# A linear-attention and gated-unit kernel: stages split by engine and issued from a table, with another order of loads

## The chip, the cores and the metric

One NeuronCore of one Trainium2 chip runs the whole kernel. The metric is device time in microseconds (us), the median over runs. A profiled run also has a span, from its first to its last instruction; the device time is some 1.8 us longer (109.45 for a span of 107.7). PE is the matmul engine (PEld its weight loads), DVE the Vector engine, ACT the Scalar engine, POOL is GpSimd, SP the engine that issues the transfers.

A run counts as slow when it is over 1.5% above the fastest of the same kernel; ratios use fast runs alone. To evacuate a result means here to copy it from where PE leaves it into a tile that the next step reads.

## The reference

A recurrent attention (state decayed by `w`, bonus `u`) over 768 steps, 4 batches and 8 heads of 48, then a gated unit with a causal convolution of width 5:

```python
for t in range(S):
    cur = einsum('bhd,bhe->bhde', u * kt, vt)
    y[:, :, t] = einsum('bhd,bhde->bhe', rt, state + cur)
    state = w * state + einsum('bhd,bhe->bhde', kt, vt)
# x = y as [batch, seq, 384]
gate = sigmoid(causal_conv5(x, conv_w))
out  = (gate * (x @ w_val)) @ w_out          # float32
```

## The kernel before

The sequence is cut into twelve units of 256 tokens (three per batch), each of two chunks of 128. A unit loads r, k, v (393 KB each), scales r and k by powers of the decay, transposes them on PE, makes the attention matrix A (`attn`) and masks it, the bonus scalars s and dv = s * v, the state, and then the output `y_out`. I call the start of that output **Y** of the unit. Convolution, gate, value and projection of a unit follow its Y, mixed with the next unit's attention.

Every engine executes its instructions in the order in which the program emits them. A stage function emits the PE work and at once its evacuation or its product:

```python
    def transp_r(n, ps=(0, NP)):
        ...                                   # 8 PE transposes into tr
        nc.scalar.copy(out=st["rT", n]..., in_=tr)
    def mask_at(n, cl):
        for par in range(2):
            nc.vector.tensor_tensor(out=st["at", n, cl][:, par], ..., op=ALU.mult)
    def bonus_v(n):
        nc.gpsimd.tensor_tensor(out=dv_t[n % 2]..., in0=v_st[n]..., in1=st["s", n]..., op=ALU.mult)
```

The start-up is written out by hand, with `warm` matmuls (results thrown away) to keep the PE clock up. The loads come first in the order r0 k0 v0 k1 r1 k2 Wv v1 Wo r2 k3 v2 r3 k4 v3 (Wv, Wo: weights). The part between Y of unit 1 and Y of unit 2:

```python
    y_out(1)
    project(0, 8)                             # the second number: warming matmuls
    conv(1)
    scale_k(3, nc.gpsimd)
    transp_r(2)
    prod(2)
    value(1, 6)
    for cl in range(U):
        attn(2, cl, 6 - 6 * cl)
        mask_at(2, cl)
    bonus(2)
    bonus_v(2)
    transp_k(3)
    ...
    state(2, 0, 6)
    ...
    # units 3 to 12: a loop of the same calls; all stores come after the last load
```

## Time and profile before

| | before |
|---|---|
| device time, median of 3 (lowest, highest) | 109.53 us (109.05, 109.62) |
| Y of units 0, 1, 2, 3, 11 | 15.83, 24.39, 38.07, 45.99, 98.72 us |
| span of the profiled run | 107.7 us |

(The prediction dates units 2 and 3 by the chain of waits, 0.07 us later than PE's own timeline does.)

The prediction below shows the page's busy sums, the chain and the stretches. Two more views say what happens in the long gap between Y of units 1 and 2. First the totals of who waited for whom (engine, line and tile that waited, what it waited for: us in all, times, longest):

```profile
POOL dv L327 <- DVE s_sb L324: 25.8, 7, 8.1
DVE pr L298 <- ACT rT L253: 13.0, 11, 3.2
```

Then the timeline in that gap (start, length, engine, line, operation; in brackets the idle time before and what ended it):

```profile
30.31 0.69 DVE L298 TENSOR_TENSOR pr<-tr_ps,rT 128x1024 bf16<-128x1024 bf16 x1 [3.15 <-ACT rT L253]
...
30.92 1.01 DVE L500 TENSOR_TENSOR hT<-at_ps,gate 128x384 bf16<-128x384 f32 x2
...
31.85 2.47 DVE L355 TENSOR_TENSOR at<-at_ps,mask 128x512 bf16<-128x512 f32 x4
...
34.24 0.17 DVE L324 COPY s_sb<-kv_ps 128x16 f32<-128x16 f32 x1
...
34.48 2.12 POOL L327 TENSOR_TENSOR dv<-v_st,s_sb 128x768 bf16<-128x768 f32 x1 [8.14 <-DVE s_sb L324]
```

DVE idles 3.15 us for the evacuated r of unit 2. Then the gated value, four masks and s stand in line, and POOL has waited 8.14 us for that s. Those waits are one queue in program order.

The long wait of POOL is not the one that ends last, though: dv was done at 36.60, and the chain of waits goes from s over PE alone to Y of unit 2:

```profile
34.32 0.09 DVE s_sb L324
34.46 0.80 PE kv_ps L138 x6
...
35.93 0.85 PE at_ps L248 x8
36.78 1.36 PE at_ps L516 x6
38.14 1.26 PE mm_ps L414 x80
```

PE ran this part cold: its granted clock was 0.50 from 34.03 to 37.44 us, and the last two pieces before Y (the transposes of r3 and a projection) took 0.85 and 1.36 us, where the steady units show 0.45 and 0.97.

### The profile page before, as it was taken

To read this page: it belongs to the slowest core of one execution; us is meant where nothing else is said; L and a number is where in the kernel's file an instruction comes from. 1 tells how busy PE (TensorE), PEld (TensorE's weight loads), DVE (VectorE), ACT (ScalarE), POOL (GpSimd) and SP (SyncE) were. 2 spreads that over 40 slices of the span, in tenths; PEclk is the share of its full clock that TensorE was granted. 3 is DMA by queue.
4 is the path that set the end of the run, shared out by engine and by line. 5 is a ranking of instruction groups with operands and counts; after the bars stand their busy time and mean duration, and the time that the engine had idled before them with its cause. 6 is when DMAs were issued, how large, how long until landed. Compare 5 with 4: busy or idle time off the path is not lost.

```text
span 107.7 us, 5253 instructions
## 1 busy us (share of the span) xinstructions
PE 94.0 (87%) x2320; PEld 76.4 (71%) x2320; DVE 71.3 (66%) x137; ACT 73.2 (68%) x120; POOL 61.1 (57%) x62
## 2 busy tenths in 40 slices
PE   4999559979965979797999999999999999999860
PEld 4696447857844768586788797788978788785720
DVE  4295894789079326876689496975968789595030
ACT  4179556694826396495787987779878796973540
POOL 7851959077001990695945959679297894105000
PEclk9999999999998599999999999999999999999996
DMA  0999998989889899897979869797999994040404
GB/s 9 224 213 224 215 287 213 312 142 195 173 154 217 164 239 193 178 246 148 245 147 226 159 114 262 139 252 156 238 245 328 359 366 138 10 152 0 152 0 146
DMA packets 67347, 20.41 MB, mean 190 GB/s; under 512 B 63478, under 2 KB 67324, under 8 KB 67324
## 3 DMA queue, kind: packets, MB, share of 16 engines
q1 hardware_dynamic: 66492, 20.07, 79.6%
q8 instruction: 18, 0.29, 1.2%
q10 hardware_dynamic: 832, 0.00, 0.4%
q14 instruction: 5, 0.04, 0.1%
HBM read 15.35 MB, written 4.72 MB: 186 GB/s over the span
## 4 chain that ended last, share of the span: by engine, by line
PE 59%; ACT 11%; DVE 10%; DMA 8%; issue 5%; SPq 3%; DVEq 0%
PE mm_ps L462 11%; PE mm_ps L414 10%; PE at_ps L516 10%; DMA r_st<-in_r_dram 8%; DVE at L355 6%; ACT rT L253 5%; PE at_ps L248 5%; PE at_ps L483 5%; PE at_ps L342 4%; PE kv_ps L373 3%; PE tr_ps L284 3%; ACT xT L442 3%; PE kv_ps L382 2%; PE at_ps L492 2%; SPq L71 2%
## 5 line engine op out<-in xcount | busy, mean ns | idle before, releaser
L327 POOL TENSOR_TENSOR dv<-v_st,s_sb 128x768 bf16<-128x768 f32 x12 | 18.4, 1530 | 31.6 <-DVE s_sb L324 25.8
L355 DVE TENSOR_TENSOR at<-at_ps,mask 128x512 bf16<-128x512 f32 x48 | 29.9, 683 | 6.9 <-PE at_ps L342 6.9
L260 POOL TENSOR_TENSOR ks<-k_st,dk 128x768 bf16<-128x768 f32 x11 | 20.1, 1828 | 3.8 <-DMA k_st<-in_k_dram 3.8
L253 ACT COPY rT<-at_ps 128x1024 bf16<-128x1024 bf16 (+1 forms) x13 | 15.8, 1230 | 9.2 <-PE at_ps L248 9.2
L500 DVE TENSOR_TENSOR hT<-at_ps,gate 128x384 bf16<-128x384 f32 x24 | 12.5, 555 | 5.8 <-PE at_ps L492 5.5
L298 DVE TENSOR_TENSOR pr<-tr_ps,rT 128x1024 bf16<-128x1024 bf16 x11 | 7.6, 692 | 13.0 <-ACT rT L253 13.0
L289 ACT COPY kT<-tr_ps 128x1024 bf16<-128x1024 bf16 x11 | 11.1, 1012 | 6.7 <-PE tr_ps L284 6.7
L471 ACT ACTIVATE gate<-mm_ps 128x384 bf16<-128x384 f32 x24 | 10.5, 488 | 6.6 <-PE mm_ps L462 6.2
L234 POOL TENSOR_TENSOR rs<-r_st,dr 128x768 bf16<-128x768 f32 x8 | 14.6, 1830 | 0.0
L516 PE MATMUL at_ps<-wout,hT 128*128 128x384 bf16 x72 | 14.4, 334 | 0.2 <-DVE hT L500 0.2
L462 PE MATMUL mm_ps<-xT,cwd 64*64 64x256 bf16 (+1 forms) x500 | 12.7, 241 | 1.7 <-ACT xT L442 0.9
L462 PEld LDWEIGHTS <-cwd 64*64 64x64 bf16 x500 | 11.5, 106 | 3.2 <-issue 1.7
L523 ACT COPY o_sb<-at_ps 128x384 f32<-128x384 f32 x24 | 10.7, 493 | 3.6 <-PE at_ps L516 3.6
L442 ACT CAST xT<-mm_ps 128x384 bf16<-128x384 f32 x24 | 11.4, 493 | 1.8 <-PE mm_ps L414 1.3
L398 DVE TENSOR_TENSOR z<-kv_ps,wcm 128x384 bf16<-128x384 f32 x20 | 11.0, 549 | 1.5 <-PE kv_ps L382 1.5
L483 PE MATMUL at_ps<-xT,wval 128*128 128x256 bf16 x72 | 11.8, 272 | 0.0
L269 ACT CAST vb<-v_st 128x768 bf16<-128x768 f32 x12 | 10.2, 847 | 0.0
L516 PEld LDWEIGHTS <-hT 128*128 128x128 bf16 x72 | 6.3, 100 | 4.6 <-DVE hT L500 1.9
L414 PE MATMUL mm_ps<-at,vb 128*32 128x128 bf16 x384 | 9.6, 219 | 0.0
L248 PE MATMUL at_ps<-ident,rs 128*128 128x128 bf16 x96 | 8.2, 235 | 1.2 <-DVE rs L234 1.2
L342 PE MATMUL at_ps<-rT,kT 48*128 48x128 bf16 x192 | 8.1, 220 | 0.6 <-DVE hT L500 0.6
L414 PE MATMUL mm_ps<-ident,dv 128*32 128x128 bf16 x288 | 8.2, 219 | 0.0
(78 smaller groups left out, 149.8 us busy)
## 6 DMA issues: line engine op xcount, KB each, us to landing
r_st<-in_r_dram SPq DMA_DIRECT2D x12, 384.0 KB, 5.1
k_st<-in_k_dram SPq DMA_DIRECT2D x24, 192.0 KB, 5.0
v_st<-in_v_dram SPq DMA_DIRECT2D x24, 192.0 KB, 4.5
out_dram<-o_sb SPq DMA_DIRECT2D x11, 384.0 KB, 4.6
wv_st<-in_moe_w_val_dram SPq DMA_DIRECT2D x1, 576.0 KB
wo_st<-in_moe_w_out_dram SPq DMA_DIRECT2D x1, 576.0 KB, 5.5
out_dram<-o_sb SPq DMA_DIRECT2D x2, 192.0 KB, 1.9
wt<-in_w_dram ACTq DMA_DIRECT2D x2, 0.8 KB, 2.5
```

Of the source, the lines that this page charges most:

```text
L234: eng.tensor_tensor(out=rs_t[n % 2][:, :, ps[0] : ps[1], :, 0:D].rearrange("p s n a d -> p (n a) s d"), in0=r_st[n][:, hs], in1=dr[:, hs], ...
L248: nc.tensor.transpose(tr[:, s, p, :], rs_t[n % 2][:, s, ps[0] + p].rearrange("p a x -> p (a x)"), ident,)
L253: nc.scalar.copy(out=st["rT", n][:, ps[0] : ps[1], :].rearrange("x n (i s) -> x s n i", s=2), in_=tr,)
L260: eng.tensor_tensor(out=ks_t[n % 3][:, cs, :, :, 0:D].rearrange("p c n a d -> p c (n a) d"), in0=k_st[n][:, cs], in1=dk[:, None, :, :].to_ ...
L327: nc.gpsimd.tensor_tensor(out=dv_t[n % 2].rearrange("p c (h d) -> p (c h) d", d=D), in0=v_st[n].rearrange("p c h d -> p (c h) d"), in1=st[ ...
L355: nc.vector.tensor_tensor(out=st["at", n, cl][:, par], in0=st["at_ps", n, cl][par], in1=mask[:, None, :].to_broadcast([128, NP, 128]), op= ...
L414: nc.tensor.matmul(out=y_ps[32 * q : 32 * q + 32, T, :], lhsT=lt, rhs=rh, start=q not in first, stop=last, skip_group_check=True,)
L442: nc.scalar.copy(out=xT_t[b % 2][:, :, t0 : t0 + C], in_=y_ps)
L462: nc.tensor.matmul(out=g_ps[i][64 * qo : 64 * qo + 64, o0 : o0 + n0], lhsT=cwd[rows, T, t, :], rhs=xT[rows, T, t0 + c0 + t : t0 + c0 + t + ...
L483: nc.tensor.matmul(out=v_ps[:, 0:W], lhsT=wval[:, kt, i, :], rhs=xT[:, kt, t0 : t0 + W], start=(kt == 0), stop=(kt == NT - 1), skip_group_ ...
L500: nc.vector.tensor_tensor(out=hT[:, i], in0=v_ps, in1=st["gate", n][:, i], op=ALU.mult)
L516: nc.tensor.matmul(out=o_ps, lhsT=hT[:, i, c0 : c0 + C], rhs=wout[:, k, :], start=(j == 0), stop=(j == 2),)
```

## The change

The intent is to separate what each stage does on each engine, so that a table of tokens can place the PE part, the evacuation and the product independently, and to load r2 early. `RT:2.0` is the transposes of r of unit 2, `RE:2.0` their evacuation, `M:2.3` the fourth mask, and so on. A name ending in D (`DVD`) runs on DVE instead of POOL; by this r of unit 2 goes from DVE to POOL. The diff, cut to its core:

```diff
-    load_kv(1, "k")
-    load_r(1)
-    load_kv(2, "k")
 ...
     def transp_r(n, ps=(0, NP)):
         ...
+        st["r_tr", n, ps[0]] = tr
+
+    def evac_r(n, ps=(0, NP)):
         nc.scalar.copy(...)
 ...                                            (every stage is cut in this way)
+    LOADS = """
+        r0 k0 v0 r1 r2 k1 k2 Wv v1 Wo k3 r3 v2 r4 v3 k4 k5 r5 v4 v5 r6 k6 v6 r7 k7 k8 v7 r8 k9 v8
+        r9 k10 v9 r10 k11 v10 r11 v11
+    """
+    HEAD = """
+        CV:0.0 PR:0.0 A:0.1 M:0.3 S:0.0 RSD:1.0 RS:2.0 SE:0.0 M:0.2 A:0.0 KV:0.0~20 TL:0.0 ZE:0.0
+        RT:1.0 M:0.1 RT:2.0 RE:1.0 KS:1.0 RE:2.0 KV:0.1 ID:0.1 DVD:0.0 KT:1.0 KS:2.0 WV:0.0 ZE:0.1
+        Y:0.1 M:0.0 KE:1.0 Y:0.0 PR:1.0 YE:0.1 YE:0.0 A:1.1 S:1.0 C:0.0 A:1.0 KT:2.0 M:1.3 SG:0.0
 ...
+    STEP = """
+        Y:-1.0 Y:-1.1 A:0.0 YE:-1.0 RS:1.0 A:0.1 M:0.0 YE:-1.1 CV:0.0 C:-1.0 M:0.1 S:0.0 SG:-1.1
+        M:0.2 KS:1.0 M:0.3 SG:-1.0 V:-1.1 RT:1.0 V:-1.0 SE:0.0 KV:0.0 ID:0.0 HT:-1.1 KT:1.0
+        HT:-1.0 RE:1.0 O:-1.0 DV:0.0 ZE:0.0 KV:0.1 O:-1.1 ID:0.1 KE:1.0 OE:-1.0 ZE:0.1 OE:-1.1
+        PR:1.0
+    """
 ...
+    def issue():
+        while loads:
 ...
+                if old >= 0 and any((e, old, 0) not in seen for e in need):
+                    return
 ...
+        while stores and {("OE", stores[0], 0), ("OE", stores[0], 1)} <= seen:
+            store(stores.pop(0))
```

Of the 71 warming matmuls 20 remain (`KV:0.0~20`). Units 0 to 3 are in HEAD; STEP is repeated for each later unit; a short TAIL ends it.

## The prediction

> **What bounds the kernel now.** I read the page first, then the chain of waits in order of time, then busy time by stretch, then the timeline. The work comes in twelve units of 256 tokens. I date a unit by the start of its first output matmul (L414, called Y below).
>
> From the page of the kernel before: busy sums, then busy tenths in 40 slices of 2.69 us.
>
> ```profile
> PE 94.0 (87%) x2320; PEld 76.4 (71%) x2320; DVE 71.3 (66%) x137; ACT 73.2 (68%) x120; POOL 61.1 (57%) x62
> ...
> PEclk9999999999998599999999999999999999999996
> DMA  0999998989889899897979869797999994040404
> ```
>
> PE is fullest, yet DMA is at eight or nine tenths from 11 us until about 88 us. So two resources are near their limit, and an average cannot say which binds where. The clock dips in one place only (32 to 38 us).
>
> The chain of waits in order of time separates the stages (start, length, what). This is its middle:
>
> ```profile
> 29.08 1.20 ACT rT L253
> 30.35 0.57 issue
> 30.92 0.31 DVE hT L500
> ...
> 31.93 0.78 DVE at L355 x2
> 32.71 0.33 issue
> 33.04 1.28 DVE at L355 x2
> ...
> 73.37 1.23 PE mm_ps L414 x80
> 74.60 0.55 PE at_ps L342 x16
> 75.18 1.02 PE mm_ps L462 x40
> ```
>
> From about 46 us to 99 us the chain is almost unbroken PE. Near 30 us it hops between ACT, DVE and issue: PE waits there for results. The timeline gives Y of unit 0 at 15.83, unit 1 at 24.39, unit 2 at 38.14, unit 3 at 46.06 and unit 11 at 98.72 us. Hence gaps of 8.56, 13.75 and 7.92 us, then eight units in 52.66, or 6.58 us each, and 8.98 us of tail. Busy time in the last four of these stretches (us and its sum, PE, PEld, DVE, ACT, POOL, clock, DMA share, GB/s):
>
> ```profile
> 24.39:38.14 13.75, 11.51 (x228) 8.90 (x231) 8.18 (x12) 7.15 (x11) 5.61 (x4) 0.88 0.87 183
> 38.14:46.06 7.92, 6.71 (x192) 5.52 (x195) 4.65 (x9) 5.55 (x10) 4.10 (x4) 1.00 0.95 207
> 46.06:98.72 52.66, 51.12 (x1437) 42.41 (x1436) 40.87 (x78) 41.71 (x72) 36.22 (x22) 1.00 0.81 199
> 98.72:107.70 8.98, 4.96 (x159) 3.54 (x158) 1.05 (x2) 3.37 (x8) 0.00 (x0) 0.89 0.25 89
> ```
>
> PE is 97% busy in the steady stretch (51.12 of 52.66) and only 84% in the one before unit 2, at a clock of 0.88, with throwaway warming matmuls inside. Three units from 15.83 to 46.06 take 30.2 us where three steady ones take 19.7: **the start-up wastes some 10 us**, and the 13.75 us gap has most of it.
>
> **What the Trainium skill says.** (1) "TensorE: Matmul & The Clock Gate", HAM oscillation: an idle PE falls back to half clock after a window of about 3.4 us. The trace agrees in kind: the stretch from 32 to 40 us shows PEclk 0.79 after PE had waited on DVE. (2) "SBUF — State Buffer", Who interferes with whom: a Vector instruction with two SBUF inputs contends with a GpSimd one. The trace agrees: the r scaling on DVE took 2.04 to 2.19 us beside POOL work and 0.95 us where POOL was idle. (3) "DMA: Bandwidth & Descriptors", Why small descriptors are slow. The page of before has 63478 of 67347 packets under 512 B; the loads ran at 204 to 229 GB/s when the DMA share was 1.00, but 80 to 86 us, mostly stores, moved 334.
>
> **The change, part by part.**
>
> *Removed:* 51 of the 71 warming matmuls (4+8+3+3+3+4+10+10+8+6+6+6 = 71 by the trace's count of L138, 20 remain in one place). They cost 4.9 us of weight loading over the kernel (L138: 71 at 103 ns, many overlapped), but most lay in waits. I credit 1 us, and it may be eaten by a colder clock.
>
> *Added:* nearly no work. The first unit's and unit 2's bonus product (dv) go from POOL to DVE, r of unit 3 from DVE to POOL. One dv on POOL is 1.48 us, and on DVE I estimate 1 to 2 us from the r scaling of the same size. Unit 0's is near the path, but PE waits for a load there anyway.
>
> *Moved, loads:* same bytes, new order. Before: r0 k0 v0 k1 r1 k2 Wv v1 Wo r2 k3 v2 r3. After: r0 k0 v0 r1 r2 k1 k2 Wv v1 Wo k3 r3 v2. One load is 393 KB; at 204 to 229 GB/s that is 1.7 to 1.9 us. k1 slips two slots, k2 one, v2 one; r2 comes far ahead, r3 one slot. In the trace the scaling of k1 started at 11.00 and of k2 at 15.40, both having waited for their loads. So k1 lands at about 15 and k2 at 17.5. Scaling k1 (1.83 on POOL) ends near 17, and the transposes of k1 stand ahead of Y on PE: **Y of unit 0 slips from 15.8 to about 17.5.** Unit 1 then waits for Wv and v1, whose places are unchanged: Y of unit 1 at about 24.2 against 24.39, no gain.
>
> *Moved, stages:* now the gap before unit 2. In the old order PE sits in line: transposed r of unit 2, its evacuation (to 30.3), bonus product, gated value, four masks (to 34.3), s, then dv on POOL (34.48 + 2.12), then Y. In the new table r of unit 2 is scaled and transposed before unit 1, attention of unit 2 stands right after Y of unit 1, and masks run under conv and projection. PE's own work there, by the lengths on the chain: A 0.55, C 1.02, O 0.97, S 0.28, V 1.00, r transposes 0.45, KV 0.17, k transposes 0.47, ID 0.16 = 5.1 us. So PE allows Y of unit 2 at 25.5 + 5.1 = 30.6. v2 sets about the same: issued at 19.98 to 23.59, landing some 4.5 later, near 28; one slot later near 30; plus cast (0.85) or dv on DVE, **31.5 to 33 instead of 38.1.** Unit 3 has one unit of PE work (6.6) plus some waits for v3, r4 and k4: 7.5 to 8.5. **Y of unit 3 at 40.5, against 46.06: a gain of 5.5 us.**
>
> *Steady loop:* by the same lengths a unit is Y 1.23 + A 0.55 + C 1.02 + S 0.28 + V 1.00 + r 0.45 + k 0.47 + KV 0.34 + ID 0.32 + O 0.97 = 6.63; every third saves 0.33 and another 0.33: 6.41 on average against 6.58 measured. The table can recover at most 1.4 us; I take 0.7, so 52.0.
>
> *Tail:* same chain of stages: 9.0.
>
> Sum: 40.5 + 52.0 + 9.0 = 101.5 us span. The profiled run took 109.45 for a span of 107.7, so add 1.75: **103.3, which I round to 103.5 us**.
>
> **The rivals.** *DMA becomes the bound.* Its queue took 79.6% of 16 engines' span, 86 us. Before, all loads came first and the stores waited (from 77.69 us). After, stores go out whenever the next loads still lack buffers; by the table four of them (units 0 to 3) precede the last v. They add 4 x 393 KB / 334 GB/s = 4.7 us of DMA. At 212 GB/s from 24 us on (4.95 MB moved by then), r11 lands near 77 us; my schedule wants it near 78. So the transfers just keep up. Against it: DMA share was only 0.81 to 0.95 in several stretches before, since the queue waited for buffers, which now come free sooner. If it binds, the end comes 1 to 4 us later: 105 to 107. *The colder PE.* Without warming matmuls PE has little to do from 12 to 17 us while k1 comes in. A half-clock window of 3.4 us costs at most 1.7 us, perhaps twice: 105 to 106.5. For it: the dip before came after just such waits. Against it: the path there is loads, not PE. *The gap merely moves:* PE executes in order, so any late load in the table (r3, v2, r4, k4) stops everything behind it. If Y of unit 2 comes at 36, the result is 107 to 108.5, nearly the same time. *The upside:* all waits hidden and a steady 6.41: about 100.5 to 101.
>
> **Range and chances.** The saving in the gap before unit 2 follows from dependencies, not from tuning luck, and survives one rival at a time. All three together would eat it. Range 101.0 to 107.5. Faster than 107.3 by over 2%: 0.86; within 2%: 0.11; slower: 0.03.
>
> **What the changed profile would show.** Right: Y of units 0, 1, 2, 3 near 17.5, 24, 32, 40.5; k1's scaling waiting for its load until about 15; four or so stores interleaved before the last v; a steady unit of 6.4 to 6.6; the tail unchanged. Wrong: PEclk well under 1 over two or more slices in the first 40 us; PE waits on r, k or v late in the run (DMA bound); or a gap before unit 2 still over 11 us. What would break the prediction most is a load landing far later than its slot, since the new table has several loads ahead of in-order PE work.

## The result, and the profile after

The changed kernel took 104.66 us (median of the 3 fast runs, 104.6 to 105.6; a fourth, 106.38, was slow) against 109.53: ratio 0.9594, 95% interval 0.9501 to 0.9686, so faster. A ratio here is the mean time of one kernel's fast runs over that of the other's of the same rounds, so not quite the ratio of the medians. The profiled execution is the one of 105.6 us.

From the page after, the lines that answer to those of before:

```profile
PE 91.0 (88%) x2269; PEld 73.2 (71%) x2269; DVE 70.6 (68%) x137; ACT 73.5 (71%) x120; POOL 61.7 (59%) x62
...
PEclk9999999999999999999999999999999999999997
DMA  0999999989997998989899798999899995400404
...
q8 instruction: 17, 0.28, 1.1%
```

In this execution the dip of the clock is gone although 51 warming matmuls are gone too. Busy time by stretch, cut at Y of units 1 and 2, at 40.00 (0.46 us after Y of unit 3) and at 94.77 (0.07 us after Y of unit 11):

```profile
22.62:30.67 8.05, 7.01 (x188) 5.56 (x188) 6.11 (x11) 5.61 (x10) 3.98 (x4) 1.00 0.95 201
30.67:40.00 9.33, 8.47 (x226) 6.44 (x229) 6.60 (x12) 7.21 (x13) 6.06 (x4) 1.00 0.94 194
40.00:94.77 54.77, 51.77 (x1423) 42.11 (x1413) 40.33 (x77) 42.76 (x71) 35.59 (x22) 1.00 0.86 209
94.77:103.80 9.03, 4.89 (x158) 3.55 (x158) 1.05 (x2) 3.29 (x8) 0.00 (x0) 0.93 0.25 89
```

The first of these lines is the one to compare with 13.75 us before: 8.05 us, at full clock. Where the 3.9 us of span went, from the Y times of the two timelines:

| stretch | before | after | difference |
|---|---|---|---|
| start to Y0 | 15.83 | 16.66 | +0.83 |
| Y0 to Y1 | 8.56 | 5.96 | -2.60 |
| Y1 to Y2 | 13.68 | 8.05 | **-5.63** |
| Y2 to Y3 | 7.92 | 8.87 | +0.95 |
| Y3 to Y11 | 52.73 | 55.16 | **+2.43** |
| Y11 to end | 8.98 | 9.10 | +0.12 |
| span | 107.7 | 103.8 | -3.90 |

So the start-up gave back 6.45 us up to Y of unit 3, and the steady units took 2.43 of it away. The timeline shows what the start-up waits for now:

```profile
12.31 1.97 POOL L230 TENSOR_TENSOR rs<-r_st,dr 128x768 bf16<-128x768 f32 x1 [3.93 <-DMA r_st<-in_r_dram]
...
24.40 0.62 PE L347 MATMUL at_ps<-rT,kT 48*128 48x128 bf16 x16
...
28.92 0.83 ACT L268 CAST vb<-v_st 128x768 bf16<-128x768 f32 x1 [1.18 <-DMA v_st<-in_v_dram]
...
30.33 1.83 POOL L230 TENSOR_TENSOR rs<-r_st,dr 128x768 bf16<-128x768 f32 x1 [2.33 <-DMA r_st<-in_r_dram]
```

Attention of unit 2 (second line) now starts 1.8 us after Y of unit 1, where the old order let it start at 30.72, 6.3 us after. What is left of long waits are those for transfers: r2 at 12.3, v2 at 28.9, r4 at 30.3 us. That the start-up is now bound by its loads is not shown: in the gap PE is busy for 7.01 of the 8.05 us, and of the waits for loads only that for v2 reaches it there (0.63 us at 29.80, through the cast of v2).

In the steady units after, 1.60 us is one stop of PE in the middle of a convolution, which waited for nothing that the profile shows (the kernel before has one stop of 0.79 us, so that 1.62 of the +2.43 us is left):

```profile
81.69 0.93 PE L463 MATMUL mm_ps<-xT,cwd 64*64 64x256 bf16 x33
84.22 0.30 PE L463 MATMUL mm_ps<-xT,cwd 64*64 64x128 bf16 x7 [1.60 <-issue]
```

The kept traces tell what such stops are, though no view of `prof` does. Counted over all runs, PE stopped 19 times for 0.46 us or more after 38 us with nothing awaited, in 12 of the 14 traces. The number of PE instructions recorded before the one that resumes is always 193 more than a multiple of 256 (3777 here), whatever that instruction does. The page's "instruction" queue (17 packets of 16384 bytes in this execution, for some 4550 PE instructions) starts a packet 2.2 to 3.0 us before each of these stops ends (here at 81.95 us, 2.27 before). The reading that fits all 19 is that PE stood still at the border of a block of 256 instructions until the next block had come. No run varied this, and why most borders cost nothing stays open.

### The profile page after: what moved, and what is told of

It reads as the page before. It is cut to its first block, busy times and chain, and to the rows that moved or that the text cites. A ratio compares the mean times of both kernels' runs of the same rounds, so it can differ in the third digit from the quotient of the medians.

```text
span 103.8 us, 5143 instructions
## 1 busy us (share of the span) xinstructions
PE 91.0 (88%) x2269; PEld 73.2 (71%) x2269; DVE 70.6 (68%) x137; ACT 73.5 (71%) x120; POOL 61.7 (59%) x62
## 4 chain that ended last, share of the span: by engine, by line
PE 42%; DVE 8%; issue 6%; ACT 1%; DVEq 0%
PE mm_ps L412 9%; PE at_ps L519 9%; PE mm_ps L463 6%; DVE at L360 4%; PE at_ps L485 4%; DVE hT L507 4%; PE at_ps L347 3%; PE at_ps L244 2%; PE tr_ps L283 2%; PE at_ps L494 2%; PE kv_ps L376 2%; PE kv_ps L387 2%; PE kv_ps L317 2%; ACT o_sb L532 1%; ACT xT L444 0%
## 5 line engine op out<-in xcount | busy, mean ns | idle before, releaser
L332 POOL TENSOR_TENSOR dv<-v_st,s_sb 128x768 bf16<-128x768 f32 x10 | 14.8, 1476 | 19.9 <-DVE s_sb L329 17.2
L230 POOL TENSOR_TENSOR rs<-r_st,dr 128x768 bf16<-128x768 f32 x10 | 18.4, 1840 | 8.5 <-DMA r_st<-in_r_dram 6.3
L507 DVE TENSOR_TENSOR hT<-at_ps,gate 128x384 bf16<-128x384 f32 x24 | 13.0, 552 | 6.5 <-PE at_ps L494 5.8
L519 PE MATMUL at_ps<-wout,hT 128*128 128x384 bf16 x72 | 15.2, 328 | 1.1 <-DVE hT L507 0.8
L519 PEld LDWEIGHTS <-hT 128*128 128x128 bf16 x72 | 5.7, 98 | 4.9 <-DVE hT L507 2.0
L494 PE MATMUL at_ps<-xT,wval 128*128 128x128 bf16 x72 | 8.1, 218 | 0.2 <-issue 0.2
```

Of the source, the lines that this page charges most:

```text
L230: eng.tensor_tensor(out=rs_t[n % 2][:, :, ps[0] : ps[1], :, 0:D].rearrange("p s n a d -> p (n a) s d"), in0=r_st[n][:, hs], in1=dr[:, hs], ...
L332: eng.tensor_tensor(out=dv_t[n % 2].rearrange("p c (h d) -> p (c h) d", d=D), in0=v_st[n].rearrange("p c h d -> p (c h) d"), in1=st["s", n ...
L507: nc.vector.tensor_tensor(out=st["hT", n][:, i], in0=st["v_ps", n, i], in1=st["gate", n][:, i], op=ALU.mult)
L519: nc.tensor.matmul(out=o_ps, lhsT=hT[:, i, c0 : c0 + C], rhs=wout[:, k, :], start=(j == 0), stop=(j == 2),)
```

## The experiments

Twelve kernels ran, all with correct results, on the same numbered chip. All Y times are from one profiled execution each, and those of one kernel differ by some 1 us between executions (Y0 of the unchanged changed kernel: 16.66 and 17.94).

| kernel | median us | ratio (95% interval) | Y0, Y1, Y2, Y3, Y11 |
|---|---|---|---|
| after_again | 104.56 | 0.9542 (0.9451, 0.9633) | 17.94, 23.60, 31.81, 40.68, 96.42 (slow run) |
| before_new_loads | 115.64 | 1.0588 (1.0489, 1.0687) | 19.70, 29.30, 43.45, 51.36, 104.16 |
| after_old_loads | 115.22 | 1.0545 (1.0492, 1.0598) | 26.54, 32.58, 39.85, 48.59, 104.16 |
| old_loads_r2_late | 108.52 | 0.9929 (0.9848, 1.0009) | 15.72, 22.00, 32.89, 41.85, 96.93 |
| before_r2_early | 115.14 | none (one fast run, 113.22) | 20.91, 30.43, 41.36, 49.39, 104.48 (slow run) |
| head_new_step_old | 104.34 | 0.9517 (0.9415, 0.9618) | 18.61, 25.77, 33.03, 41.77, 95.53 (slow run) |
| new_head_old_step_2 | 106.06 | 0.9546 (0.9442, 0.9649) | 17.89, 23.87, 31.59, 40.46, 95.18 |
| head_old_step_new | 110.18 | 1.0108 (1.0012, 1.0203) | 14.75, 23.70, 37.76, 45.68, 99.01 |
| before_no_warm | 111.33 | 1.0105 (0.9997, 1.0212) | 15.20, 23.61, 37.82, 45.74, 100.10 |
| after_no_warm | 107.57 | none (one fast run, 105.12) | 18.25, 24.50, 32.03, 40.77, 97.22 (slow run) |
| after_stores_between | 106.06 | 0.9640 (0.9548, 0.9732) | 17.29, 22.94, 31.25, 40.12, 95.54 |
| after_dv0_pool | 104.62 | 0.9549 (0.9466, 0.9633) | 17.68, 23.66, 30.93, 39.77, 93.91 |

Does the new framework change anything but orders? `head_old_step_new` below has the old start-up written as a table in it. Its trace shows the instructions of the kernel before in the same order on all five engines until the steady order sets in (on PE for 859 matmuls, to 48.9 us).

### Is it the loads or the stages?

**The changed kernel again** (`after_again`, no edit).

> The changed kernel once more, as a control. Theory: 104 to 105.5 us; output matmuls of units 0, 1, 2, 3 start near 16.7, 22.6, 30.7, 39.5 us. The 1.6 us stop of PE inside a conv at 82.6 us, which waited for nothing that the profile shows, is an accident of that one run and will not stand at the same place; then the eight steady units take near 53.6 us, not 55.2. Rival: the stop belongs to the new order (it comes while the stores run), and is there again near 82 us.

Ratio 0.9542: the gain is reproduced. PE stopped at 50.48 (0.91 us), 66.18 (0.74) and 85.17 (0.78). The last of these is the stop of the first profile again, at the same instruction; Y of unit 9, and the stop with it, came 2.55 us later here:

```profile
85.94 0.30 PE L463 MATMUL mm_ps<-xT,cwd 64*64 64x128 bf16 x7 [0.78 <-issue]
```

So the stop was no accident of one run, against the theory. But it does not belong to the new steady order either: with the old one in its place (`new_head_old_step_2`) it is there at the same matmul, 0.78 us long. Where PE can stop is fixed; whether it stops there, and for how long, is not. Y3 to Y11 took 55.74, less 2.43 of stops 53.3 us: the steady units are slower than before even without them.

**New loads, old stages** (`before_new_loads`).

```diff
     load_r(0); load_kv(0, "k"); load_kv(0, "v")
-    load_kv(1, "k"); load_r(1); load_kv(2, "k")
+    load_r(1); load_r(2); load_kv(1, "k"); load_kv(2, "k")
     ...
-    load_r(2); load_kv(3, "k"); load_kv(2, "v"); load_r(3); load_kv(4, "k"); load_kv(3, "v")
+    load_kv(3, "k"); load_r(3); load_kv(2, "v"); load_r(4); load_kv(3, "v"); load_kv(4, "k"); load_kv(5, "k")
```

> The kernel before with nothing changed but the order of its first loads (r2 ahead of k1, r3 ahead of v2 and so on). Theory: the gain needs the stages of unit 2 to be moved; the new load order alone only delays k1, so the output of unit 0 slips by about 1 us and the gap before unit 2 stays over 12 us: 109.5 to 111 us. Rival: the loads set the head, and the new order alone brings 3 us or more: 106.5 us or less.

The direction was right and the size far off: 115.64 us, 6% slower. POOL of this run shows why:

```profile
15.71 1.80 POOL L261 TENSOR_TENSOR ks<-k_st,dk 128x768 bf16<-128x768 f32 x1 [7.33 <-DMA k_st<-in_k_dram]
17.47 1.47 POOL L328 TENSOR_TENSOR dv<-v_st,s_sb 128x768 bf16<-128x768 f32 x1
```

In the old order the scaling of k1 stands ahead of dv of unit 0 on POOL, so the delay of k1 by 4.7 us (11.00 to 15.71) goes whole into dv. PE meanwhile waits 3.4 us for k1, its granted clock over 12 to 17.5 us falls to 0.55, and stays near half (0.52) over the next 5.5 us. Y of unit 0 stands behind the transposes of k1 and r1 on PE and comes at 19.70, and the gap to unit 1 grows to 9.6 us.

**Old loads, new stages** (`after_old_loads`): only the line of loads is put back.

```diff
-        r0 k0 v0 r1 r2 k1 k2 Wv v1 Wo k3 r3 v2 r4 v3 k4 k5 ...
+        r0 k0 v0 k1 r1 k2 Wv v1 Wo r2 k3 v2 r3 k4 v3 r4 k5 ...
```

> The changed kernel with the old load order; stage table unchanged. Theory: in the table the scaling of r2 stands ahead of that of k1 on POOL, and engines work in order, so everything waits for r2, which now lands near 22 to 23 us: output of unit 0 at 25 us or later and a time of 110 to 114 us. Rival: the order of the loads hardly matters beside that of the stages: 104.5 to 106 us.

115.22 us, slower still than the theory's 110 to 114; Y of unit 0 came at 26.54, as it said. POOL waits for r2 and blocks k1 behind it:

```profile
21.95 1.80 POOL L230 TENSOR_TENSOR rs<-r_st,dr 128x768 bf16<-128x768 f32 x1 [13.57 <-DMA r_st<-in_r_dram]
```

Either half of the change, put in alone like this, costs 5 to 6%; together they gain 4 to 5%.

**Old loads, new stages but r2's late** (`old_loads_r2_late`): `RS:2.0 RT:2.0 RE:2.0` are moved to just ahead of `A:2.0`.

> The changed kernel with the old load order, and the scaling, transposes and evacuation of r2 put just ahead of the attention of unit 2 in the table so that nothing waits for it early. Theory: most of the gain is that masks, bonus product and gated value of the units interleave; r2's own place costs only some waits near 23 to 28 us: 105 to 107 us. Rival: having r2 ahead of k1 is what the gain rests on: 108 us or more.

108.52 us, ratio 0.9929: over the theory's range and in the rival's (108 or more), so most of the gain in time does rest on the early r2 with its load. Y1 to Y2 took 10.89 us: without the early r2 the new stages take some 2.8 of the 5.6 us out of the gap. (The 26 warming matmuls in it are gone too, but `before_no_warm` lacks them in the old order and had 14.21 us there.) Y of unit 3 comes at 41.85, already 4.1 us ahead of the kernel before; 2.4 us of that are lost again up to Y of unit 11.

**Old stages with r2 early** (`before_r2_early`, on top of `before_new_loads`):

```diff
-    scale_k(1, nc.gpsimd)
     bonus_v(0)
+    scale_r(2, nc.gpsimd)
+    scale_k(1, nc.gpsimd)
     ...
     transp_r(1)
+    transp_r(2)
     ...
-    scale_r(2, nc.vector)
     ...
-    transp_r(2)
```

> The kernel before with the new first loads, and r2 scaled on POOL behind dv of unit 0 and transposed right after r1; all else in the old order. Theory: dv of unit 0 is out of the way of k1, so unit 0 does not slip as with the new loads alone (17 to 18 us instead of 19.7), and with r2 ready the gap before unit 2 falls from 14 us to 10 to 12 us, since the old order still has four masks, s and dv in line: 108 to 111 us, ratio 0.985 to 1.015. Rival: r2 was the whole obstacle and the gap falls to 8 us: ratio 0.96 to 0.97.

Y1 to Y2 fell to 10.93 us as the theory said, so an early r2 alone is also worth some 2.8 us there (against 13.68; 3.2 against the 14.15 of `before_new_loads`, on which it is built). Both this and `old_loads_r2_late` ran the gap at full clock and the kernel before at 0.88, so part of each saving is the clock that no longer falls there. The total missed it: Y of unit 0 came at 20.91, not 17 to 18, because the transposes of k1 still stand ahead of it on PE, which waited 4.06 us for them and then ran at a lowered clock. With a single fast run the time has no interval. It suggests, and no run isolates it, that the early r2 pays only if PE has something to do until k1 comes; in the new table the transposes of r1 and r2 and the 20 warming matmuls stand there.

### What became of the steady units?

**New start-up, old steady order** (`head_new_step_old`, run twice; the second time as `new_head_old_step_2`): STEP and TAIL are replaced by the old loop written as tokens.

```diff
-        Y:-1.0 Y:-1.1 A:0.0 YE:-1.0 RS:1.0 A:0.1 M:0.0 ... V:-1.1 RT:1.0 V:-1.0 ... HT:-1.1 KT:1.0 HT:-1.0 ...
+        Y:-1.0 YE:-1.0 Y:-1.1 YE:-1.1 CV:0.0 KS:1.0 A:0.0 ... KT:1.0 KE:1.0 V:-1.0 HT:-1.0 V:-1.1 HT:-1.1 ...
```

> The changed kernel's loads and start-up table, then the old order of stages for the steady units and the tail. Theory: the new steady order is the worse one (free of its stops the changed kernel took 53.3 to 53.6 us for eight units, the old one 51.7), so this one is faster than the changed kernel by 1 to 2 us: 102 to 103.5 us, ratio to before 0.935 to 0.948. Rival: the two steady orders cost the same, and the difference is what the stops of PE leave: ratio 0.950 to 0.960 as the changed kernel has.

> The new loads and start-up with the old steady order, once more, because the first five rounds left open whether it beats the changed kernel. Theory: 1 us better than the changed kernel: ratio 0.938 to 0.950, and the eight steady units, less the stops of PE, 51.5 to 52.5 us. Rival: no difference: ratio 0.950 to 0.958.

**Old start-up, new steady order** (`head_old_step_new`): the reverse.

> The old loads and start-up order, then the new order of stages for the steady units and the tail. Theory: slower than before by 1 to 2 us: 110.5 to 111.5 us, ratio 1.005 to 1.02, output of unit 3 at 46 us as before. Rival: the new steady order is equal or better: ratio 0.99 to 1.0.

The steady stretch, Y3 to Y11, less the stops of PE (pieces of the chain called issue of over 0.6 us), in every profiled execution but two (`after_stores_between` waited for loads, and the clock of `before_r2_early` dipped inside the stretch):

| steady order | Y3 to Y11 less stops, us | mean |
|---|---|---|
| old: before, before_new_loads, before_no_warm, head_new_step_old, new_head_old_step_2 | 51.94, 52.80, 52.51, 52.33, 52.43 | 52.4 |
| new: after, after_again, after_old_loads, old_loads_r2_late, head_old_step_new, after_no_warm, after_dv0_pool | 53.56, 53.31, 54.10, 53.37, 53.33, 53.91, 53.34 | 53.6 |

The two groups do not overlap: in the traces the new steady order costs some 1.2 us. The time of `head_old_step_new` agrees (ratio 1.0108, interval above 1). The kernels with the new start-up and the old steady order do not confirm it in time: 0.9517 and 0.9546 against 0.9542, intervals of a per cent either way, and PE stops of 1.4 and 2.3 us in the two profiled runs. That they beat the changed kernel is not shown.

Where the new order loses is seen best in the last unit before the tail, 5.97 us before and 6.29 after. The gated value (hT) and the projection there, before and then after:

```profile
96.89 1.01 DVE L500 TENSOR_TENSOR hT<-at_ps,gate 128x384 bf16<-128x384 f32 x2
...
97.50 1.29 PE L516 MATMUL at_ps<-wout,hT 128*128 128x384 bf16 x6
```

```profile
92.55 1.01 DVE L507 TENSOR_TENSOR hT<-at_ps,gate 128x384 bf16<-128x384 f32 x2
...
93.62 1.15 PE L519 MATMUL at_ps<-wout,hT 128*128 128x384 bf16 x6 [0.42 <-DVE hT L507]
```

Before, the projection starts 0.61 us after the first half of hT has begun. After, it starts 1.07 us after, when both halves are done. The table makes half 1 of hT first (`HT:-1.1` ahead of `HT:-1.0`), yet each projection's first matmul reads half 0. That the swapped halves are the cause follows from the code and this timing; swapping them back was not run. It is a part of the loss only: less the stops, each of the eight units is slower, by 0.06 to 0.34 us, and the last one by 0.32.

### The rivals of the prediction

**Stores among the loads** (`after_stores_between`): one word, `return` to `break`, so that stores need not wait until all loads are issued.

> The changed kernel with the first four stores placed among the last loads (one ahead of k10, two ahead of r10, one ahead of r11), as the prediction had wrongly read the table; the changed kernel holds all stores behind the last load. Theory: the queue keeps up either way, since r11 is used some 5 us after it lands: ratio to before 0.950 to 0.960, as the changed kernel. Rival: the stores delay r10 and r11, the r scaling on POOL waits for its loads near 72 and 79 us, and 1 us or more is lost: ratio over 0.963.

Here the rival's waits came, 4 us later than it said; its ratio, over 0.963, was met barely, and the interval holds the theory's range too. Its POOL timeline:

```profile
76.41 1.81 POOL L230 TENSOR_TENSOR rs<-r_st,dr 128x768 bf16<-128x768 f32 x1 [3.02 <-DMA r_st<-in_r_dram]
...
82.92 1.82 POOL L230 TENSOR_TENSOR rs<-r_st,dr 128x768 bf16<-128x768 f32 x1 [1.49 <-DMA r_st<-in_r_dram]
```

Its chain of waits goes over that transfer:

```profile
69.81 6.44 DMA r_st<-in_r_dram
```

The unit around it took 7.86 us (74.05 to 81.91) and the whole 0.9640 of before, against 0.9549 of `after_dv0_pool` (the intervals overlap). The changed kernel itself issued its last load at 73.18 us and every store behind it, and shows no wait for a load after 31 us of 0.6 us or more (one of POOL, 2.64 us at 85.2, is put down to a store).

**No warming matmuls** (`before_no_warm`: none of the 71; `after_no_warm`: `KV:0.0~20` becomes `KV:0.0`).

> The kernel before without any of its 71 warming matmuls. Theory: they keep the clock up in the start-up; without them PEclk falls below 0.9 in more slices between 9 and 40 us and the time is 0.5 to 3 us longer: 110 to 112.5 us. Rival: they are in the way of in-order PE work, and without them it is 0.5 to 1.5 us faster: 108 to 109 us.

> The changed kernel without its last 20 warming matmuls ahead of the state of unit 0. Theory: PE is nearly idle from 11.7 to 16 us, the clock falls to half for a window near 14 to 20 us, and the time grows by 0.5 to 2 us: ratio to before 0.958 to 0.975. Rival: the loads set the pace there and nothing changes: ratio 0.950 to 0.957.

The kernel before without them: 1.0105, interval 0.9997 to 1.0212, so most likely 1% slower, as the theory said, but with two fast runs and not clear of noise; the granted clock was 0.50 from 13.65 to 17.07 and from 30.72 to 37.54 us. The changed kernel without its 20 had one fast run (105.12 us) in four; in its profiled execution PEclk stayed full although PE was busy only 4.64 of the 7 us from 11 to 18 us.

**dv of unit 0 back on POOL** (`after_dv0_pool`: `DVD:0.0` becomes `DV:0.0`).

> The changed kernel with dv of unit 0 back on POOL, in the same place of the table (behind the scaling of k1). Theory: the move to DVE was needed, because POOL waits in order for r2 and k1: output of unit 0 at 18 us or later instead of 16.7, the scaling of k2 1.5 us later, and 0.5 to 1.5 us in all: ratio 0.960 to 0.970. Rival: Wv and v1 set unit 1 anyway, and nothing is lost: ratio 0.950 to 0.958.

0.9549: no loss, the rival was right. dv ran at 17.03 us behind k1's scaling and PE waited 0.30 us for it, Y of unit 0 came at 17.68, within the spread of the unchanged kernel, and Y of unit 1 at 23.66.

## Why the prediction was right

The predicted time was 103.5 us in a range of 101.0 to 107.5; 104.66 was measured. By its own steps, against the first two profiles of the changed kernel:

- **Y of unit 0 slips to 17.5.** 16.66 in the first profile, 17.94 in the second: right. The mechanism (k1 two slots later, its transposes ahead of Y) is what `before_new_loads` shows. There it cost more: the transposes of r1 stood behind those of k1, and the clock was 0.50 from 12.56 to 22.80 us. That dv was tied to k1 as well is not the reason: it is so in `after_dv0_pool` too, with Y at 17.68.
- **Y of unit 1 at 24.2, no gain.** 22.62 and 23.60. Better by about 1 us; it seems, though no run isolates it, that Wv and v1 were not what unit 1 waited for longest.
- **The gap before unit 2.** Y at 31.5 to 33 foreseen, 30.67 and 31.81 found. Right in size, and in cause with one correction. Each of two experiments with only the early r2 or only the interleaving took about half of it, part of that being the clock. The last wait of PE before Y is for v2, as the prediction said (ACT waits 1.18 us for v2, PE 0.63 for ACT). But dv on POOL, which the prediction puts just ahead of Y in the old order, was not waited for: the chain goes over PE's own work at half clock, which it did not count.
- **Y of unit 3 at 40.5.** 39.54 and 40.68.
- **Steady units 52.0.** This step failed: 55.2 and 55.7 us were measured. The prediction took the sum of PE's lengths per unit (6.41) as a floor and gave the table half the distance to it. The new order costs about 1.2 us where 0.7 was to be gained, and stops of PE of 1.6 to 2.4 us came on top; the kernel before had 0.79 us of them. Nor is PE the only bound: in three of the eight units (from 54.66, 74.85 and 90.08 us on) the chain after goes over masks and hT on DVE. The stops are at the borders of blocks of 256 PE instructions (above), a cost that the prediction has nowhere.
- **Tail 9.0.** 9.10.
- **DMA as a rival.** The estimate that the queue "just keeps up" with four stores ahead of the last v rested on a misreading: `return` holds all stores until the loads are out. Its sum is off too: 14.95 MB of loads up to r11 and 1.57 of stores, less 4.95, take 54.6 us at 212 GB/s, so r11 lands near 78.6, not 77. Where the four stores were really put among the loads, r10 and r11 came late, by 3.0 and 1.5 us. So the change avoids a real wait; that it costs time is likely, but not clear of noise.
- **The colder PE.** Not seen in the two profiles of the changed kernel: PEclk is full in all slices but the last. But `head_new_step_old` and `new_head_old_step_2`, which are the same program up to Y of unit 3, ran at 0.50 from 16.77 to 23.60 and from 16.19 to 19.60 us. Their Y of unit 3 came at 41.77 and 40.46, against 39.54, 40.68 and 40.12 (`after_stores_between`) at full clock. So the rival does come true in some executions, and costs at most some 2 us there. In the old stages with the new loads it is seen plainly.
- **A reading of a line.** The r scaling of 0.95 us at 34.32 did not run "where POOL was idle": POOL's dv began 0.16 us after it and took 2.12 us instead of 1.48. The trace shows the contention, but there POOL was the one that waited.

In the first profile a gain of 1 us too little was foreseen up to Y of unit 3 and some 3 us too much after it; the errors partly cancelled, by luck. That execution took 105.6 us, 2.1 over the forecast; the median is within 1.2.

## What to carry to other kernels

When engines execute in program order, an order of loads and an order of stages are one decision: each half of this change alone lost 5 to 6%, both together won over 4%. (Over the old loads the new stages lost nothing once r2's stood where r2 arrives: ratio 0.9929.) Read the gaps between the same landmark of successive units; a gap twice the steady one names the place to work on, and its timeline says which queue holds it. After such a gain look again at the stretch that was good before, since a reordered inner step can quietly give a microsecond back. Before a stop is called an accident, find its place in the instruction stream: here one of 0.78 us, 2.55 us later in the run, was the same one.

## What the Trainium skill lacked or had wrong

- "Runtime: NRT & Kernel Launch", Instruction fetch mechanics, says that the sequencer fetches its next block of instructions through a DMA queue of its own and that crossing a block border is mostly hidden. In 12 of the 14 traces here it was not always: PE stopped for 0.46 to 1.93 us, up to three times from 38 us on, always at a border of 256 PE instructions and until 2.2 to 3.0 us after a packet of the instruction queue had started. The section does not say when a border is not hidden.
- "DMA: Bandwidth & Descriptors", Bandwidth, measures transfers by total size and has no rate for a stream of rows of 192 and 384 bytes. Here such loads ran at 204 and 216 GB/s in the two stretches of the kernel before (66 to 73 and 46 to 53 us) with nothing else in them and a DMA share of 1.00 or more, and 6 us of almost only stores of 1536-byte rows (80 to 86) at 334.
- "TensorE: Matmul & The Clock Gate", HAM oscillation, speaks of idle gaps longer than a window. It agrees with 0.55 of the clock over 12 to 17.5 us of `before_new_loads`, where PE was busy 1.65 of 5.5 us. It gives no share of busy time below which the clock falls. In the kernel before it fell at 34.03 us after 3.41 us in which PE had been busy for 1.85 and never idle for 1 us at a time; in `after_again` it stayed full from 12.30 to 19.13 us, with 1.73 and 1.84 us busy in the two halves.
